# Sparse attention with a gated feed-forward network: the scores of six steps formed eight steps ahead and kept in DRAM

## The chip, the cores and the metric

One core of one Trainium2 chip runs the whole program. The metric is the device time in microseconds of one execution; the kernel before was run three times, and the median of these is the time before.

## The reference

```python
def _attn_ref(q, k, v):                      # (8, 8, 576, 64) each
    scores = scale * np.matmul(q, k.transpose(0, 1, 3, 2))
    kth = np.partition(scores, -32, axis=-1)[..., -32:-31]
    scores = np.where(scores >= kth, scores, -1e9)
    attn = np.exp(scores - np.max(scores, axis=-1, keepdims=True))
    attn = attn / (np.sum(attn, axis=-1, keepdims=True) + 1e-09)
    return np.matmul(attn, v)

def _moe_ref(x, w_gate, w_val, w_out):       # x (4608, 512), 512 -> 1536 -> 512
    gate = 1.0 / (1.0 + np.exp(-(x @ w_gate)))
    return gate * (x @ w_val) @ w_out
```

In each row of the scores only the 32 largest of 576 count; the output of all heads goes through the feed-forward network.

## The kernel before, in words

The attention is cut into 160 steps. A step is 128 rows of a pair of heads (two score rows of 576 per partition), or the last 64 rows of both heads. Steps are numbered n = 0, 1, ...; the first batch has steps 0 to 7 (row tiles 0 and 1 of the four pairs of heads), 8 to 15 (tiles 2 and 3) and 16 to 19 (the rest). In the names of tiles, `s_2_1` is tile 2 of pair 1, which is step 10; steps 10 to 15 are `2_1`, `3_1`, `2_2`, `3_2`, `2_3`, `3_3`.

A step goes through these stations. `begin` (L633) runs `scores` (L300): two groups of matmuls `pss` on TensorE (L310), each into the one buffer of the PSUM pool `ps_s`, and after each an eviction to `s` by ScalarE (L314). `select` (L389) finds a threshold on VectorE: `cand` (L407) and `tops` and `leads` (L412, L414) take the 24 largest; from the last of these ScalarE marks in `under` (L422) what is below it, GpSimd multiplies the marks into `u` (L429, closed by L430), and VectorE takes `kths` (L437), the 32nd value. ScalarE forms the exponentials `e` (L344), VectorE masks and sums them (L349). `turn` (L440) transposes them on TensorE (`pt`, L448) with evictions to `ring` (L454), `weigh` (L478) multiplies by the values (`po`, L496).

Beside this runs the feed-forward network in float32 split into a high and a low part. Its weights are loaded raw (`wraw`), split once on ScalarE, VectorE (`wbits`, `wpower`, L203 to L205), GpSimd (`wsplit`, L209) and TensorE (`wrest`, L217 to L219), and written to DRAM, from where later units read them.

The loop of `run` (L616) writes, for every n, the matmuls of the scores of step n + 2, of the transposes of step n - 2 and of the feed-forward network in chunks; TensorE keeps exactly this order. The order on the other engines and on SyncE's queue is made by a scheduler from the program. Up to `OPEN` = 9 there is no feed-forward work to interleave; the first weights are split then. Scores have four buffers (`bs`), so the scores of step n + 4 go where step n's lay, once step n is masked.

Of the kernel before, what the change touches and what calls it, by code (L numbers as in the profile page):

```python
# [10 lines left out]
F32 = mybir.dt.float32  # L11
# [6 lines left out]
AF = mybir.ActivationFunctionType  # L18
# [5 lines left out]
SHRINK = 2.0**-60  # L24
# [6 lines left out]
def tile_topk_attention_then_gated_ffn(  # L31
# [8 lines left out]
    nc = tc.nc  # L40
    P = 128
    B, H, _, S = k.shape
    D = P // 2
    HALF = S // 2
    NP = H // 2
# [3 lines left out]
    FG = NE = NP  # L49
    NF = 2 * n_w // 3  # L50
    NG = NF // FG
    SCALE = 1.0 / 8.0
# [9 lines left out]
    groups = [(b, half) for b in range(B) for half in (halves[b % 2] if b else opening)]  # L62
# [6 lines left out]
    def size(i):  # L69
        return P if i < NT else REM  # L70
# [12 lines left out]
    WHOLE = 1  # L83

    OPEN = NP * 2 + 1
    PINNED, BACK = 3, 6
    KEPT = 3

# [13 lines left out]
    dram = ctx.enter_context(tc.tile_pool(name="dram", bufs=1, space=bass.MemoryType.DRAM))  # L102
# [21 lines left out]
    pools = {}  # L124
# [24 lines left out]
    def urgent():  # L149
        return tc.high_priority() if stated else ExitStack()  # L150

    for name, bufs in (("w", 3), ("f2", 3), ("f4", 3), ("fg", FG + 1)):
        pools[name] = ctx.enter_context(tc.tile_pool(name=name, bufs=bufs))


    order = list(range(FG))
# [4 lines left out]
    stored, splits, waiting, fetched, ticks, evicted, due, later, pinned, raw_loads = set(), {}, [], {}, [0], [], [], [], [], []  # L161
# [10 lines left out]
    def load(dst, src_, late=False):  # L172
        with tc.issue_after(raw_loads[max(0, len(raw_loads) - BACK)]) if late and raw_loads else ExitStack():
            ins = nc.sync.dma_start(dst, src_)
        if pinned:
            tc.keep_in_program_order(ins)
        return ins
# [54 lines left out]
    def first_weights(at):  # L232
        for t in order[at : at + 3]:
            if t in fetched:
                continue
            if t in order[:KEPT]:
                fetched[t] = splits[t]
                continue
            if t in stored:
                fetched[t] = stored_weight(t, "first")  # L240
                continue
            while due:
                next_front()
            due.extend([(t, 0), (t, 1)])
            next_front()
            fetched[t] = splits[t]
# [53 lines left out]
    def scores(s, qs, ks, i, nm):  # L300

        J = 2 if i < NT else 1
        K = D if len(qs) == 1 else P
        if K == D and J == 2:
            for half in range(2):
                ps = ps_s.tile([P, 2, 512], F32, tag="s", name=f"pss_{nm}_{half}")
                c = slice(half * HALF, (half + 1) * HALF)
                for j in range(J):
                    rows = slice(j * D, (j + 1) * D)
                    nc.tensor.matmul(  # L310
                        ps[:, j, :HALF], qs[0][rows, j * P : (j + 1) * P], ks[0][rows, c], start=True, stop=True
                    )
                with urgent():
                    evicted.append(nc.scalar.activation(s[:, :, c], ps[:, :, :HALF], AF.Copy, scale=SCALE * SHRINK))  # L314
                yield
            return
        for j in range(J):
            ps = ps_s.tile([P, 2, 512], F32, tag="s", name=f"pss_{nm}_{j}")
            for half in range(2):

                parts = [(j, 0, HALF, half * HALF)]
                if i == NT:

                    m = S - REM - HALF
                    parts += [(1, 0, HALF, REM)] if half == 0 else [(1, 0, m, REM + HALF), (1, m, REM, 0)]
                todo = [(x, part) for part in parts for x in qs]
                for t, (x, (h, o, n, k0)) in enumerate(todo):
                    nc.tensor.matmul(  # L328
                        ps[:, half, o : o + n],
                        x[:K, h * P : (h + 1) * P],  # L330
                        ks[h][:K, k0 : k0 + n],
                        start=t == 0,
                        stop=t == len(todo) - 1,
                    )
            with urgent():
                nc.scalar.activation(  # L336
                    s[:, j].rearrange("p (a n) -> p a n", a=2), ps[:, :, :HALF], AF.Copy, scale=SCALE * SHRINK
                )
            yield
# [276 lines left out]
    def run(general):  # L616
# [11 lines left out]
        def fetch_values(m):  # L628
            if 0 <= m < len(steps) and steps[m][2] == groups[steps[m][0]][1][0] and steps[m][:2] not in values:
                g, p, _ = steps[m]  # L630
                values[g, p] = load_values(groups[g][0], p, f"{mark}{g}_{p}")

        def begin(m):  # L633
            if m < len(steps):
                g, p, i = steps[m]
                nm = f"{mark}{groups[g][0]}_{i}_{p}"
                staged[m] = bs.tile([P, 2, S], F32, tag="s", name=f"s_{nm}")
                yield from scores(staged[m], qs.pop(m), keys[groups[g][0], p], i, nm)

        def ask(m):  # L640
            if m < len(steps):
                g, p, i = steps[m]
                qs[m] = load_queries(groups[g][0], i, p)

# [140 lines left out]
        for n in range(len(steps) + 3):  # L785
            splitting = not general and len(fronts) > 0
            if pinned and n == PINNED:
                pinned.pop()
            if n == 0:
                fetch_keys(2)  # L790
                ask(AHEAD)
            if splitting:
                split_front(*fronts.pop(0))
            if n == OPEN and not general:
                first_weights(0)
            if n == 0:
                for m in (1, *range(3, KEYS)):
                    fetch_keys(m)
                for m in range(AHEAD + 1, ASK):
                    ask(m)  # L800
            if later and (general or n >= 2 * NP):
                load(*later.pop(0))
            fetch_values(n if n < starts[GATHER - 1] else n - 2)
            fetch_keys(n + KEYS)
            ask(n + ASK)
            goal = 0 if n < OPEN else max(at - BEHIND, np.interp(at, *zip(*PACE))) * per_row
            first = begin(n + AHEAD)
            second = turned(n - 2) if 2 <= n < len(steps) + 2 and (general or n != OPEN) else iter(())
            if region is None:
                for _ in first:  # L810
                    pass
                choose(n)
                more(goal)
                for _ in second:
                    pass
                if 2 <= n < len(steps) + 2:
                    weighed(n - 2)
            else:
                if n == OPEN - 1:
                    weighed(n - 3)  # L820
                if n == OPEN:
                    weighed(n - 3)
                    weighed(n - 2)
                choose(n)
                if n == OPEN + 1:
                    del standing["cand"], standing["tops"]
                    opened.clear()
                if n == OPEN + NP:
                    standing.clear()
                third = iter(())  # L830
                chunks = [first, second, second, first, None, second]
                if n == OPEN - 1:
                    third = turned(n - 1)
                    chunks = [second, second, second, first, third, third, third, first]
                if n == OPEN:
                    chunks = [first, None, None, first]
                begun = work
                for t, chunk in enumerate(chunks):
                    ticks[0] += 1
                    if not fronts and not splitting:  # L840
                        if waiting and ticks[0] - waiting[0][4] > 3:
                            split_back()
                        if due and len(waiting) < 3:
                            next_front()
                    if chunk is not None:
                        next(chunk, None)
                        while unfinished and t == 0:
                            weighted(*unfinished.pop(0))
                    elif 3 <= n:
                        weighed(n - 3)  # L850
                    if t == 2 and splitting and len(waiting) > 1:
                        split_back()
                    if n != OPEN or t > 0:
                        more(begun + (goal - begun) * (t + 1) / len(chunks))
                for _ in third:
                    pass
                for chunk in (first, second):
                    for _ in chunk:
                        pass
            if 2 <= n < len(steps) + 2:  # L860
                at += size(steps[n - 2][2]) / NP
# [77 lines left out]
```

## Time and profile before

| what | value |
|---|---|
| time, median of three runs (lowest to highest) | 1569.1 us (1567.16 to 1569.84) |
| the profiled execution's own time | 1569.45 us |
| its span, first to last instruction | 1567.7 us |
| TensorE matmuls busy | 1502.3 us, 96% |
| TensorE weight loads busy | 1311.4 us, 84% |
| VectorE busy | 1289.9 us, 82% |
| ScalarE busy | 1149.4 us, 73% |
| GpSimd busy | 1106.3 us, 71% |
| mean granted clock of TensorE | 0.989 |

The span leaves 1.75 us of the own time outside. Busy shares are means over stages: a stage has its own fullest engine, and time is lost or won there.

### The profile page before, as it was taken

How to read it: one execution, taken by the hardware profiler on the slowest of the kernel's cores; microseconds unless marked ns; L12 is line 12 of the kernel's file. 1: busy time of each engine (PE TensorE's matmuls, PEld its weight loads, DVE VectorE, ACT ScalarE, POOL GpSimd, SP SyncE). 2: the span in 40 equal slices, each digit the busy share in tenths (PEclk: the TensorE clock that was granted, in tenths of full speed). 3: DMA queues.
4: the chain of work that ended last, by engine and by line, in shares of the span. 5: the costliest groups of instructions: out<-in, count | busy, mean ns of one | idle time of the engine just before them, and what ended most of it. 6: DMA issues, size and time to landing. Idle time of an engine off the chain costs nothing.

```text
span 1567.7 us, 33618 instructions
## 1 busy us (share of the span) xinstructions
PE 1502.3 (96%) x10242; PEld 1311.4 (84%) x10242; DVE 1289.9 (82%) x5996; ACT 1149.4 (73%) x2519; POOL 1106.3 (71%) x1656
## 2 busy tenths in 40 slices
PE   5688999999999999999999999999999999999998
PEld 2355668988898899888898899888898899889897
DVE  7999987899999788999989788999988788998001
ACT  6888987888777777787777777787777778776221
POOL 4758897698786876897676876887675876774312
PEclk9899999999999999999999999999999999999999
DMA  6436888777665675665565676575565676564575
GB/s 204 152 123 220 280 285 299 257 269 271 229 221 192 231 268 202 207 241 205 199 213 192 230 271 207 204 253 205 199 211 191 229 248 207 197 214 169 210 272 185
DMA packets 96239, 347.34 MB, mean 222 GB/s; under 512 B 13104, under 2 KB 33584, under 8 KB 68272
## 3 DMA queue, kind: packets, MB, share of 16 engines
q1 hardware_dynamic: 90864, 326.22, 60.3%
q10 hardware_dynamic: 5184, 18.88, 3.1%
q8 instruction: 83, 1.36, 0.3%
q14 instruction: 108, 0.88, 0.2%
HBM read 316.60 MB, written 28.45 MB: 220 GB/s over the span
## 4 chain that ended last, share of the span: by engine, by line
PE 68%; DVE 15%; POOL 7%; ACT 6%; issue 3%; DMA 2%; SPq 0%; ACTq 0%; POOLq 0%; DVEq 0%
PE pz L557 10%; PE pz L558 10%; PE pz L559 10%; PE po L496 8%; PE pss L328 8%; PE pt L448 6%; PE po L581 5%; PE po L582 5%; PE po L583 5%; DVE e L349 3%; POOL u L429 3%; DVE cand L407 3%; DVE kths L437 3%; POOL wsplit L209 1%; ACT under L422 1%
## 5 line engine op out<-in xcount | busy, mean ns | idle before, releaser
L429 POOL TENSOR_TENSOR u<-s,under 128x288 f32<-128x288 f32 x576 | 425.3, 762 | 128.1 <-ACT under L422 123.3
L557 PE MATMUL pz<-xh,w 128*128 128x384 f32 (+1 forms) x1152 | 404.4, 351 | 0.0
L407 DVE MAX8 cand<-s 128x8 f32<-128x72 f32 x2304 | 353.4, 217 | 38.8 <-ACT s L336 26.7
L559 PE MATMUL pz<-xh,w 128*128 128x384 f32 (+1 forms) x1152 | 377.4, 328 | 0.0
L558 PE MATMUL pz<-xl,w 128*128 128x384 f32 (+1 forms) x1152 | 376.9, 327 | 0.0
L422 ACT ACTIVATE under<-s,leads 128x576 fp8e4<-128x576 f32 x288 | 222.4, 773 | 102.3 <-DVE leads L412 94.0
L349 DVE SCALAR_TENSOR_TENSOR e<-s,kths,e 128x576 f32<-128x576 f32 x288 | 282.4, 987 | 14.8 <-ACT e L344 14.4
L437 DVE MAX8 kths<-u 128x8 f32<-128x584 f32 x288 | 219.3, 762 | 71.0 <-POOL u L430 68.5
L569 POOL TENSOR_TENSOR gl<-gf,gh 128x384 fp32r<-128x384 f32 (+1 forms) x156 | 156.6, 1004 | 120.3 <-ACT gh L568 117.4
L557 PEld LDWEIGHTS pz<-xh,w 128*128 128x128 f32 x1152 | 217.0, 188 | 5.6 <-DVE tops L412 1.1
L344 ACT ACTIVATE e<-s,st 128x576 f32<-128x576 f32 x288 | 208.9, 770 | 16.0 <-PE pt L448 8.5
L558 PEld LDWEIGHTS pz<-xl,w 128*128 128x128 f32 x1152 | 217.7, 189 | 0.8
L559 PEld LDWEIGHTS pz<-xh,w 128*128 128x128 f32 x1152 | 216.5, 188 | 0.0
L454 ACT ACTIVATE ring<-pt 128x384 f32<-128x384 f32 x336 | 163.1, 495 | 56.2 <-PE pt L448 54.8
L448 PE MATMUL pt<-ident,e 128*128 128x128 f32 x1152 | 192.0, 276 | 6.9 <-ACT ring L454 6.9
L448 PEld LDWEIGHTS pt<-ident,e 128*128 128x128 f32 x1152 | 147.5, 142 | 38.7 <-ACT ring L454 10.5
L581 PE MATMUL po<-w,gh 128*128 128x512 f32 x408 | 173.1, 424 | 1.2 <-DVE gf L567 1.2
L336 ACT ACTIVATE s<-pss 128x576 f32<-128x576 f32 x256 | 164.0, 641 | 9.1 <-PE pss L328 8.5
L328 PE MATMUL pss<-k,qh 128*128 128x288 f32 (+2 forms) x588 | 162.2, 294 | 8.6 <-ACT s L336 8.4
L582 PE MATMUL po<-w,gl 128*128 128x512 f32 x408 | 161.2, 395 | 2.8 <-POOL gl L569 2.8
L567 DVE SCALAR_TENSOR_TENSOR gf<-gf,pz 128x384 f32<-128x384 f32 (+1 forms) x156 | 79.7, 511 | 99.9 <-PE pz L559 87.8
L583 PE MATMUL po<-w,gh 128*128 128x512 f32 x408 | 161.2, 395 | 0.0
(114 smaller groups left out, 3314.0 us busy)
## 6 DMA issues: line engine op xcount, KB each, us to landing
w<-ws SPq DMA_DIRECT2D x216, 1024.0 KB
v<-in_v_dram SPq DMA_DIRECT2D x68, 320.0 KB
wraw<-in_w_dram SPq DMA_DIRECT2D x36, 512.0 KB
ws<-wsplit ACTq DMA_DIRECT2D x36, 512.0 KB
qraw<-in_q_dram SPq DMA_DIRECT2D x140, 128.0 KB
kraw<-in_k_dram SPq DMA_DIRECT2D x56, 288.0 KB
out_dram<-acc SPq DMA_DIRECT2D x36, 256.0 KB
invb<-rows SPq DMA_DIRECT2D x66, 128.0 KB
```

What stands on the lines that cost most here:

```text
L328: nc.tensor.matmul(ps[:, half, o : o + n], x[:K, h * P : (h + 1) * P], ks[h][:K, k0 : k0 + n], start=t == 0, stop=t == len(todo) - 1,)
L349: nc.vector.scalar_tensor_tensor(e[:, j], s[:, j], kth[j], e[:, j], op0=ALU.is_ge, op1=ALU.mult, accum_out=st[:, 4 + j : 5 + j])
L407: nc.vector.max(cand[:, j, 8 * g : 8 * g + 8], s[:, j, g * SEG : (g + 1) * SEG])
L429: nc.gpsimd.tensor_tensor(u[:, j, c], s[:, j, c], under[:, j, c], op=ALU.mult)
L437: nc.vector.max(kths[:, at[j] : at[j] + 8], u[:, j])
L448: nc.tensor.transpose(pt[:, c], ef[:, k0 : k0 + P], ident)
L557: nc.tensor.matmul(ps[:, R], wt[:, u, 0, d], xh[:, R], start=d == 0, stop=False)
L558: nc.tensor.matmul(ps[:, R], wt[:, u, 0, d], xl[:, R], start=False, stop=False)
L559: nc.tensor.matmul(ps[:, R], wt[:, u, 1, d], xh[:, R], start=False, stop=d == NP - 1)
L581: nc.tensor.matmul(outs[r], gh, wh, start=f == 0, stop=False)
L582: nc.tensor.matmul(outs[r], gl, wh, start=False, stop=False)
L583: nc.tensor.matmul(outs[r], gh, wl, start=False, stop=f == FG - 1)
```

## The change

Steps 10 to 15 (`SAVED`) have their scores formed in the turns n = 2 to 7, one step's in each, eight steps ahead. `save` loads their queries into a pool of its own, runs `scores` into a pool `es` of three buffers, and stores the result to DRAM from ScalarE's queue. In the turns n = 8 to 13 `begin` reads it back into the buffer of `bs` in place of forming it, and `ask` no longer loads these queries. The chunks of the turns 2 to 7 become nine in place of six. The pools of the feed-forward network are opened at `OPEN`, where the two new pools are closed.

```diff
+    SAVED = range(OPEN + 1, OPEN + 2 * NP - 1)
...
-    for name, bufs in (("w", 3), ("f2", 3), ("f4", 3), ("fg", FG + 1)):
-        pools[name] = ctx.enter_context(tc.tile_pool(name=name, bufs=bufs))
+    pools["w"] = ctx.enter_context(tc.tile_pool(name="w", bufs=3))
+    kept = ExitStack()
+    kept_pools = {n: kept.enter_context(tc.tile_pool(name=n, bufs=bufs, side="right")) for n, bufs in (("es", 3), ("eq", 3))}
+    saved = {}
+
+    def feed_forward_pools():
+        kept.close()
+        for name, bufs in (("f2", 3), ("f4", 3), ("fg", FG + 1)):
+            pools[name] = ctx.enter_context(tc.tile_pool(name=name, bufs=bufs, side="right"))
...
+        def save(m):
+            if m in SAVED and not general:
+                g, p, i = steps[m]
+                b = groups[g][0]
+                nm = f"{b}_{i}_{p}_saved"
+                whole = kept_pools["eq"].tile([P, 2 * P], F32, tag="q", name=f"q_{nm}")
+                load(whole, q[b, i, p])
+                s = kept_pools["es"].tile([P, 2, S], F32, tag="s", name=f"s_{nm}")
+                yield from scores(s, (whole,), keys[b, p], i, nm)
+                saved[m] = dram.tile([P, 2, S], F32, tag=f"s{m}", name=f"saved_{m}")
+                nc.scalar.dma_start(saved[m], s)
...
                 staged[m] = bs.tile([P, 2, S], F32, tag="s", name=f"s_{nm}")
+                if m in saved and not general:
+                    nc.sync.dma_start(staged[m], saved.pop(m))
+                    return
                 yield from scores(staged[m], qs.pop(m), keys[groups[g][0], p], i, nm)
...
-            if m < len(steps):
+            if m < len(steps) and (general or m not in SAVED):
...
             if n == OPEN and not general:
+                feed_forward_pools()
                 first_weights(0)
...
                 chunks = [first, second, second, first, None, second]
+                early = save(n + OPEN - 1)
+                if n + OPEN - 1 in SAVED and n < OPEN - 1:
+                    chunks = [first, second, early, second, first, None, second, early, early]
```

The order of TensorE in the turn n = 4, from the first scores of step 6 (`pss_0_3_0`) to the second; `pt_0_1` are the transposes of step 2, `wrest` belongs to a weight split. Before:

```order
L310 MATMUL pss_0_3_0_663<-k_3_6_410,q_0_3_414 128x288 x2
L448 MATMUL pt_0_1_0_667<-ident,e_0_1_420 128x128 x3
L448 MATMUL pt_0_1_1_672<-ident,e_0_1_420 128x128 x3
L217 MATMUL wrest_1_677<-wbits_1_500,ident 128x512
L218 MATMUL wrest_1_677<-wsplit_395,minus 128x512
L219 MATMUL wrest_1_677<-wsplit_395,minus 128x512
L310 MATMUL pss_0_3_1_683<-k_3_6_410,q_0_3_414 128x288 x2
```

Now, where lines stand eight to ten further down:

```order
L318 MATMUL pss_0_3_0_686<-k_3_6_407,q_0_3_411 128x288 x2
L458 MATMUL pt_0_1_0_690<-ident,e_0_1_417 128x128 x3
L318 MATMUL pss_2_2_saved_698<-k_2_4_254,q_2_2_saved 128x288 x2
L225 MATMUL wrest_1_702<-wbits_1_510,ident 128x512
L226 MATMUL wrest_1_702<-wsplit_392,minus 128x512
L227 MATMUL wrest_1_702<-wsplit_392,minus 128x512
L458 MATMUL pt_0_1_1_708<-ident,e_0_1_417 128x128 x3
L318 MATMUL pss_0_3_1_713<-k_3_6_407,q_0_3_411 128x288 x2
```

The first half of the scores of step 12 stands between the two halves of step 6, in the same PSUM buffer, and one group of transposes moves behind the weight split; the second half of step 12 comes at the end of the turn.

The order of VectorE in step 7 (`1_3`), from the row after its last `leads` to its first `kths<-u_1_3`. Before:

```order
L407 MAX cand_2_0_1051<-s_2_0_875 128x8 x5
L364 RECIPROCAL st_1_2_727<-st_1_2_727 128x2
L407 MAX cand_2_0_1051<-s_2_0_875 128x8
L437 MAX kths<-u_0_3_829 128x8
L407 MAX cand_2_0_1051<-s_2_0_875 128x8 x8
L501 TENSOR_TENSOR xf_3_0_913<-po_3_902,ring 128x128 x2
L407 MAX cand_2_0_1051<-s_2_0_875 128x8 x2
L204 SCALAR_TENSOR_TENSOR wbits_0_1368<-wraw_0_924,wbits_0_1368 128x512
L437 MAX kths<-u_0_3_829 128x8
L349 SCALAR_TENSOR_TENSOR e_0_3_828,st_0_3_826<-s_0_3_662,kths,e_0_3_828 128x576
L205 TENSOR_SCALAR wpower_0_1369<-wbits_0_1368 128x512
L437 MAX kths<-u_1_3_943 128x8
```

Now, from the two `leads` of step 7 on:

```order
L422 MAX leads<-cand_1_3_996 128x8 x2
L417 MAX cand_2_0_1120<-s_2_0_922 128x8 x8
L447 MAX kths<-u_1_3_1001 128x8 x2
L211 TENSOR_SCALAR wbits_0_1423<-wbits_0_1423 128x512
L212 SCALAR_TENSOR_TENSOR wbits_0_1423<-wraw_0_984,wbits_0_1423 128x512
L213 TENSOR_SCALAR wpower_0_1424<-wbits_0_1423 128x512
L417 MAX cand_2_0_1120<-s_2_0_922 128x8 x8
```

The thresholds and the masking of step 6 have moved ahead of the `leads` of step 7, the weight split behind its `kths`; what stands between `leads` and `kths` is eight `cand`. Before, a `wbits` (L203) and a small operation stood between the two `leads` as well.

SyncE's queue after the first weights have been asked for (`w_first`). Before:

```order
L229 DMA w_first_1255<-ws_129 128x2048
L174 DMA q_3_3_1424<-in_q_dram 128x256
L174 DMA wraw_1_1489<-in_w_dram 128x1024
L174 DMA wraw_0_1517<-in_w_dram 128x1024
L174 DMA wraw_1_1573<-in_w_dram 128x1024
```

Now:

```order
L237 DMA w_first_1319<-ws_129 128x2048
L661 DMA s_2_2_1382<-saved_745 128x1152
L182 DMA wraw_1_1539<-in_w_dram 128x1024
L182 DMA wraw_0_1567<-in_w_dram 128x1024
L661 DMA s_3_2_1530<-saved_854 128x1152
L182 DMA wraw_1_1619<-in_w_dram 128x1024
L661 DMA s_2_3_1737<-saved_982 128x1152
```

The scores of steps 12, 13 and 14 are read back between the loads of raw weights; the query load has gone.

## Rows read from the trace of the kernel before

**Rows 1.** Windows: PE, PEld, DVE, ACT, POOL busy; clock, DMA share, GB/s.
```profile
20.00:95.00 75.00, 55.73 (x256) 29.37 (x256) 71.10 (x330) 59.21 (x122) 44.18 (x70) 0.89 0.52 162
95.00:180.00 85.00, 76.25 (x424) 54.11 (x421) 81.36 (x309) 74.09 (x154) 68.55 (x97) 0.96 0.65 223
180.00:240.00 60.00, 54.76 (x293) 38.81 (x292) 47.79 (x144) 49.69 (x103) 55.58 (x79) 1.00 0.79 276
240.00:1567.00 1327.00, 1307.57 (x9253) 1186.10 (x9251) 1078.16 (x5143) 955.22 (x2124) 931.96 (x1389) 1.00 0.64 223
```

**Rows 2.** Waits of VectorE, 20 to 95 us: total us, times, longest.
```profile
DVE cand L407 <- ACT s L314: 1.7, 2, 1.0
...
DVE kths L437 <- POOL u L430: 0.4, 1, 0.4
```

**Rows 3.** Waits of TensorE, 20 to 95 us.
```profile
PE pss L310 <- ACT s L314: 15.1, 7, 3.6
```

**Rows 4.** Windows, line L310 alone: PE, PEld busy; clock, DMA share, GB/s.
```profile
89.00:157.00 68.00, 9.64 (x48) 3.82 (x48) 0.95 0.53 183
```

**Rows 5.** Windows, line L314 alone: ACT busy; clock, DMA share, GB/s.
```profile
89.00:157.00 68.00, 7.11 (x11) 0.95 0.53 183
```

**Rows 6.** Timeline of TensorE: start us, us, instruction, count, idle before.
```profile
28.77 1.33 PE L310 MATMUL pss<-k,q 64*128 64x288 f32 x4 [1.93 <-ACT s L314]
...
60.24 0.76 PE L310 MATMUL pss<-k,q 64*128 64x288 f32 x4
```

**Rows 7.** Chain of waits, 14 to 302 us: start us, us, what.
```profile
23.64 0.48 DVE wbits L203
...
34.66 0.46 ACT under L422
...
40.44 0.04 DVE kths L437
...
41.12 0.41 DVE wpower L205
...
46.38 6.79 DMA wraw<-in_w_dram
...
66.71 0.67 DVE wbits L204
...
95.52 0.49 DVE xf L501 x2
96.01 1.49 DVE cand L407 x11
97.49 0.67 DVE kths L437
...
99.63 0.72 DVE e L349 x2
...
301.26 4.68 DMA w<-ws
```

**Rows 8.** Timeline of VectorE, around 92 us.
```profile
92.46 0.22 DVE L412 MAX8 leads<-cand 128x8 f32<-128x64 f32 x1
```

**Rows 9.** Timeline of ScalarE, around 93 us.
```profile
92.91 0.77 ACT L422 ACTIVATE under<-s,leads 128x576 fp8e4<-128x576 f32 x1
```

**Rows 10.** Timeline of GpSimd, 92 to 98 us.
```profile
93.84 2.67 POOL L429 TENSOR_TENSOR u<-s,under 128x288 f32<-128x288 f32 x4 [1.42 <-ACT under L422]
96.47 0.46 POOL L430 TENSOR_TENSOR u<-over,sums 128x16 f32<-128x16 f32 x2
```

**Rows 11.** Waits of VectorE, 95 to 200 us.
```profile
DVE kths L437 <- POOL u L430: 3.8, 4, 2.0
...
DVE cand L407 <- ACT s L314: 0.7, 1, 0.7
```

**Rows 12.** The page's DMA issues: count, KB each.
```profile
w<-ws SPq DMA_DIRECT2D x216, 1024.0 KB
...
wraw<-in_w_dram SPq DMA_DIRECT2D x36, 512.0 KB
```

More of the change, by code (lines that the diff above doesn't have):

```diff
@@ L313, in scores @@
                 with urgent():
-                    evicted.append(nc.scalar.activation(s[:, :, c], ps[:, :, :HALF], AF.Copy, scale=SCALE * SHRINK))
+                    out_ = nc.scalar.activation(s[:, :, c], ps[:, :, :HALF], AF.Copy, scale=SCALE * SHRINK)
+                    if not nm.endswith("saved"):
+                        evicted.append(out_)
                 yield
```

## Prediction

> **What bounds the kernel now.** I read the busy time by stage first, then who waits for whom in the first stage, then the chain of waits for durations. By stage [rows 1]: up to 20 us things fill up. From 20 to 95 us (the opening, steps 0 to 8, no feed-forward work yet) VectorE is busy 71.10 of 75 us, TensorE only 55.73. From 95 to 180 us VectorE is busy 81.36 of 85 us and TensorE 76.25. From 180 to 240 us GpSimd is the fullest, 55.58 of 60 us. From 240 us to the end TensorE is busy 1307.57 of 1327 us. So a delay or a gain that reaches 240 us passes almost whole to the end, and before it the engine to watch is VectorE: what it does not lose, no other engine can win. In the opening it hardly waits: 1.7 us in two waits for scores and 0.4 us for a threshold (`kths`) [rows 2]. TensorE waits much there, 15.1 us in seven waits, and all of it for ScalarE to empty the one PSUM buffer of scores [rows 3].
>
> **What moves.** 24 matmuls, seen as 48 records, leave the stretch from 89 to 157 us, where they take 9.64 us [rows 4], and 12 evictions with them (11 fall inside this stretch, 7.11 us [rows 5]). Both go into steps 2 to 7. A group of four records lasts 0.76 us at the full clock of 2.4 GHz and 1.33 us at 1.2 GHz [rows 6]; the granted clock in the opening is 0.89 on the mean [rows 1]. So TensorE takes on 9 to 16 us, of which 75 - 55.73 = 19.3 us are free, and ScalarE, busy 59.21 of 75 us [rows 1], about 7 us. By busy time there is room, and in the same way nothing is won behind: from 89 to 157 us the removed work lies beside a VectorE that is busy 96%. I cost the removal at nothing for that reason. If VectorE were not the cover, it would be worth up to 9.64 us (first rival).
>
> **The loss: cover on VectorE.** The order of VectorE shows the price. After the last `leads` of a step its thresholds need `under` on ScalarE and five operations on GpSimd. What VectorE has to do meanwhile is its cover. The change puts an eviction behind `under` in ScalarE's order and two more turns of the one PSUM buffer into each step, so the next step's scores come later, and in the new order VectorE stands with less to do. For step 7 before: two `leads`, 16 `cand`, two `kths`, `xf`, one `wbits` of each kind, `wpower`, one `e`, two small ones. By the chain's durations [rows 7] that is 0.3 + 16 x 1.49/11 (2.2) + 2 x 0.67 + 0.49 + 0.48 + 0.67 + 0.41 + 0.72 + 0.2 = 6.8 us. After: two `leads` and eight `cand`, 0.3 + 1.1 = 1.4 us. Worked out in the same way from the whole order, steps 4, 5, 6 have 8.8, 7.0 and 8.0 us before and 4.2, 1.4 and 2.3 us after; steps 0 to 3 keep 5.8 us or more.
>
> What the loop needs: undisturbed, `leads` starts at 92.46 us [rows 8], `under` at 92.91 [rows 9], four `u` run from 93.84 and the first closing `u` ends near 96.7 [rows 10], so 4.2 us. Disturbed by a weight split, `under` starts at 34.66 and `kths` at 40.44 us [rows 7], 5.8 us, with the 0.45 us ahead of it 6.2 us. Step 7 then waits 2.8 to 4.8 us, step 5 the same, step 6 1.9 to 3.9 us, step 4 0 to 2.0 us: together 7.5 to 15.5 us. I take values near the undisturbed end, because the new order has no weight split between the `u` of steps 5 and 7: 2.8 + 2.8 + 2.4 (step 6 has an `inv` and an eviction in between) + 1.0 (step 4, an eviction and a `wsplit`) = **+9.0 us**. The 1.7 us of waits for scores [rows 2] go, since `cand` now comes later: **-1.7 us**.
>
> **The gain behind the opening.** In steps 9 to 15 the cover grows, since scores no longer wait for TensorE's turn: from 7.5, 5.5, 9.0, 10.2, 5.0, 5.6, 4.2 to 9.5, 7.9, 11.2, 10.8, 10.0, 6.8, 6.1 us. VectorE's waits from 95 to 200 us are 3.8 us in four for `u` and 0.7 us for scores [rows 11]. At best all 4.5 us go, at worst none; with three of seven covers formerly near the 4.2 to 6.2 us needed and all above 6 now, I take **-3.4 us**.
>
> **The read-back.** Each of the six loads (576 KB) waits on SyncE's queue until the step four before has been masked, and behind it stand raw weights (the order above). The raw weights in front of it wait for VectorE too, but for splits that stand earlier in its order. From the end of `e` of step 9 to `cand` of step 13 VectorE has 4.3 us of work, from step 8 to step 12 6.4 us, for the other loads more. The trace has no such load. Nearest rows: 1024 KB of weights in 4.68 us, 512 KB of raw weights in 6.79 us [rows 7], sizes in [rows 12]. With about 0.3 us to issue, step 13 waits 0.7 to 2.8 us and step 12 up to 0.7; nothing, if a half-empty set of DMA engines (busy 0.65 [rows 1]) is quicker. I take **+0.7 us**, by the larger transfer. The Trainium skill, "DMA: Bandwidth & Descriptors", sections "Specifications" and "Anatomy of one DMA", gives some 2 us of fixed cost and 368 GB/s; an estimate from that page is 2 + 1.6 = 3.6 us, which would hide all six and make the sum 0.7 us less. The rows speak for more, but under other traffic.
>
> **At nothing.** The six stores are issued on ScalarE's queue beside its work, and land while steps 3 to 9 run. The six query loads only change places. The pools of the feed-forward network now lie where the saved scores lay, so their first writes wait for the last store, which has the whole of step 8 to land; should it be late, the first Tanh waits and TensorE behind it, a few us at most. The reads add 3.5 MB to a DMA share of 0.65 to 0.79 [rows 1].
>
> **Sum.** 9.0 - 1.7 - 3.4 + 0.7 = +4.6 us by 240 us, where TensorE takes over and passes it on. The profiled execution took 1569.45 us, 0.35 us above the median of the three runs, so the median should go from 1569.1 to **1573.7 us**. Bounds of the terms alone: from 7.5 - 1.7 - 4.5 = +1.3 us, with 3 us more taken back in the 12.2 us that VectorE idles from 180 to 240 us [rows 1] -1.7 us, to 15.5 - 0 + 3.5 = +19 us, with all four steps disturbed at once, which I think rare.
>
> **Rivals.** (1) *Faster.* The stretch from 89 to 240 us is limited by TensorE and ScalarE after all, and VectorE is only kept busy by an order that follows them. It decides if the covers of steps 4 to 7 cost less than the relief. For it: TensorE is busy 76.25 of 85 us and VectorE stands in the chain only in turns with others. Against it: 96% busy. Price: the 9.64 us [rows 4] at most, and half of it if the other half lies beside other work as now, so about -5 us without the loss and 1564 us. The Trainium skill, "Perfetto Trace Analysis", section "Optimization Strategy", says that kernels with several regimes may gain from interleaving them, which is what is done here; by that rule the time falls, the rows say that both regimes share VectorE. 13%.
> (2) *No change.* The added waits of the opening are given back whole, because VectorE's idle time, 3.6 us from 95 to 180 and 12.2 us from 180 to 240 us [rows 1], take them up: 1569. 13%.
> (3) *Much slower.* The one PSUM buffer becomes the bound of the opening: 12 more turns at the 15.1/7 = 2.2 us that a turn waits now [rows 3] are 26 us, of which the 4 us of TensorE's idle time that are no such wait, and half of the rest, hide; about +12 us, 1581. For it: ScalarE's order puts evictions behind `under`, which waits for VectorE. Against it: VectorE reaches the next `cand` after its wait for `kths`, by when the scores are out. The Trainium skill, "Perfetto Trace Analysis", section "Matmuls", wants matmul groups to rotate through PSUM banks so that evictions overlap, and speaks against adding groups here; the 15.1 us agree. 14%.
> That the change does not do what it says I rule out: the order shows the matmuls in their new places.
>
> **Numbers.** The forecast holds 60%: of that 48 slower by over 0.2% (3.1 us, about what a measurement of this kernel can tell from no change) and 12 within it. With the rivals: faster 13%, within 25%, slower 62%. Range 1566 to 1582 us: it takes in the forecast, no change, most of the third rival and the nearer part of the first.
>
> **What would show it.** VectorE's waits for `u` in the first 105 us rise from 0.4 to some 9 us, by about 2.5 us a step in steps 5 to 7, with the boundary at 95 us about 7 us later; from there to 200 us they nearly vanish; `cand` of step 13 waits for a DMA by about 1 us; TensorE's first full slice comes about 5 us later. The forecast is wrong if VectorE's idle time in the opening stays under 5 us, or if the stretch from the first feed-forward matmul to 240 us shrinks by more than 6 us.

## The result and the profile after

The changed kernel takes 1592.2 us (median, 1590.5 to 1593.7) against 1569.2 us for the kernel before on the same chip: ratio 1.0149, 95% interval 1.0131 to 1.0166, so 23.1 us slower. The forecast was 1573.7 us, with a range of 1566 to 1582: the direction was right, the loss five times as large. The profiled execution took 1591.46 us, its span is 1589.4 us.

Where the time went is told by the places where VectorE scales a finished weighing (`xf`). The last one of the opening starts at 115.48 us, before at 95.52 [rows 7]: 20.0 us later. Behind it, a place that both traces show is a run of ten score matmuls (`pss` x10) in the stretch where TensorE is full: it starts at 262.73 us, before at 241.24, 21.5 us later. The whole span is 21.7 us longer. So nearly all of the loss arises in the opening, and nothing is given back behind it.

Windows of the changed kernel, with the columns of [rows 1]:

```profile
20.00:116.00 96.00, 66.46 (x302) 34.43 (x303) 72.32 (x333) 68.45 (x135) 43.13 (x72) 0.80 0.57 183
116.00:200.00 84.00, 67.10 (x366) 49.74 (x366) 78.78 (x304) 65.66 (x136) 66.01 (x95) 0.92 0.69 233
200.00:262.00 62.00, 57.35 (x306) 41.35 (x305) 50.38 (x147) 52.48 (x110) 56.38 (x82) 1.00 0.83 282
```

VectorE does the same work up to the boundary, 72.32 us against 71.10 in [rows 1], but in 96 us where it had 75. Its waits in that stretch (us in all, times, longest):

```profile
DVE xf L511 <- PE po L507: 9.1, 2, 8.3
DVE kths L447 <- POOL u L440: 7.5, 3, 2.9
DVE cand L417 <- ACT s L322: 4.7, 2, 4.0
DVE wbits L211 <- ACT wbits L209: 1.7, 1, 1.7
```

They add up to 23.0 us. Before, up to 96 us, so that the wait ahead of the last `xf` of the opening is counted there too, the 1.7 us for `cand` and 0.4 for `kths` of [rows 2] stand beside

```profile
DVE xf L501 <- PE po L497: 1.8, 2, 1.2
...
DVE wbits L203 <- ACT wbits L201: 0.3, 1, 0.3
```

which makes 4.2 us. The difference in waiting, 18.8 us, and the 1.2 us of more work (72.32 - 71.10) are the 20.0 us by which the boundary moved: VectorE is the engine to watch, as the prediction had it, but little more than a third of its new waits (7.5 - 0.4 = 7.1 us) is the one that was forecast. Their places, in VectorE's timeline (start, us, instruction, in brackets the idle time ahead):

```profile
40.02 1.18 DVE L417 MAX8 cand<-s 128x8 f32<-128x72 f32 x8 [3.97 <-ACT s L322]
...
67.62 0.77 DVE L447 MAX8 kths<-u 128x8 f32<-128x584 f32 x1 [2.91 <-POOL u L440]
...
79.36 0.77 DVE L447 MAX8 kths<-u 128x8 f32<-128x584 f32 x1 [1.94 <-POOL u L440]
...
91.50 1.57 DVE L447 MAX8 kths<-u 128x8 f32<-128x584 f32 x2 [2.60 <-POOL u L440]
...
106.59 0.49 DVE L511 TENSOR_TENSOR xf<-po,ring 128x128 f32<-128x128 f32 x2 [8.26 <-PE po L507]
```

The three `kths` are those of steps 5, 6 and 7. The other two, 12.2 us together, wait for work that comes out of TensorE. What TensorE waited for up to 116 us:

```profile
PE pss L318 <- ACT s_saved L322: 15.4, 5, 5.3
PE pss_saved L318 <- ACT s L322: 7.7, 8, 2.5
PE pss L318 <- ACT s L322: 5.2, 2, 2.6
```

That is 28.3 us for the one PSUM buffer of scores, against 15.1 in [rows 3]. The largest single one shows how it comes about. TensorE's timeline, and then ScalarE's in the same place:

```profile
40.04 0.76 PE L318 MATMUL pss_saved<-k,q_saved 64*128 64x288 f32 x4 [0.16 <-ACT s L322]
46.12 1.33 PE L318 MATMUL pss<-k,q 64*128 64x288 f32 x4 [5.33 <-ACT s_saved L322]
```

```profile
39.34 0.65 ACT L322 ACTIVATE s<-pss 128x576 f32<-128x576 f32 x1 [0.65 <-PE pss L318]
39.88 0.66 ACT L209 ACTIVATE wbits<-wraw 128x512 f32<-128x512 f32 x1
40.44 0.66 ACT L215 ACTIVATE wsplit<-wraw 128x512 fp32r<-128x512 uint32 x1
40.98 0.60 ACT L464 ACTIVATE ring<-pt 128x512 f32<-128x512 f32 x1
41.46 0.78 ACT L432 ACTIVATE under<-s,leads 128x576 fp8e4<-128x576 f32 x1
...
42.22 0.78 ACT L432 ACTIVATE under<-s,leads 128x576 fp8e4<-128x576 f32 x1
...
42.98 1.45 ACT L354 ACTIVATE e<-s,st 128x576 f32<-128x576 f32 x2
44.31 0.67 ACT L209 ACTIVATE wbits<-wraw 128x512 f32<-128x512 f32 x1
44.87 0.67 ACT L215 ACTIVATE wsplit<-wraw 128x512 fp32r<-128x512 uint32 x1
45.43 0.64 ACT L322 ACTIVATE s_saved<-pss_saved 128x576 f32<-128x576 f32 x1
```

The saved half is done at 40.8 us, but its eviction stands in ScalarE's order behind seven operations that start only after that (from `ring` to the last `wsplit`), and runs at 45.43. Until then the buffer is full, the next step's own half can't start, and the transposes and weighings behind it in TensorE's order stand too. The same pattern makes the 8.26 us; in the chain of waits (start, us, what):

```profile
97.18 0.55 ACT s_saved L322
...
97.77 0.78 PE pss L318 x4
...
98.58 0.66 ACT s L322
...
99.28 0.76 PE pss_saved L318 x4
100.03 1.07 PE wrest L225 x2
...
101.13 0.68 ACT wbits L209
...
102.70 0.66 ACT s L322
...
103.40 0.76 PE pss_saved L318 x4
104.16 0.36 PE po L506
```

The one buffer is handed on from a saved half to an own half to a saved half, each time through ScalarE, and `po`, which VectorE waits for, comes behind the last of them.

### The profile page after: what moved, and what is told of

It is laid out like the page before. It is cut to its first block, busy times and chain, and to the rows that moved or that the text cites. A ratio compares the mean times of both kernels' runs of the same rounds, so it can differ in the third digit from the quotient of the medians.

```text
span 1589.4 us, 33647 instructions
## 1 busy us (share of the span) xinstructions
PE 1506.2 (95%) x10242; PEld 1314.3 (83%) x10242; DVE 1292.5 (81%) x5996; ACT 1153.0 (73%) x2519; POOL 1103.3 (69%) x1656
## 4 chain that ended last, share of the span: by engine, by line
PE 65%; DVE 17%; POOL 7%; ACT 5%; issue 3%; DMA 3%; SPq 0%; POOLq 0%; DVEq 0%; ACTq 0%
PE pz L567 10%; PE pz L569 9%; PE pz L568 9%; PE pss L338 7%; PE po L506 7%; PE pt L458 5%; PE po L591 5%; PE po L593 5%; PE po L592 5%; DVE e L359 4%; DVE cand L417 4%; DVE kths L447 3%; POOL u L439 3%; DVE cand L424 1%; DMA wraw<-in_w_dram 1%
## 5 line engine op out<-in xcount | busy, mean ns | idle before, releaser
L359 DVE SCALAR_TENSOR_TENSOR e<-s,kths,e 128x576 f32<-128x576 f32 x288 | 285.8, 999 | 14.4 <-ACT e L354 13.9
```

Of the source, the lines that this page charges most:

```text
L359: nc.vector.scalar_tensor_tensor(e[:, j], s[:, j], kth[j], e[:, j], op0=ALU.is_ge, op1=ALU.mult, accum_out=st[:, 4 + j : 5 + j])
```

## The experiments

The theory after the result (A): the loss is made in the opening, by the turns of the one PSUM buffer, through ScalarE's order; the work removed behind the opening was worth nothing. Its rivals: the extra evictions or matmuls themselves, the place of the saved halves in the order, the stores or the read-back, and single steps that cost more than the others. Each run's difference is taken to the kernel before on the same chip (in the table's order: 1569.15 us for the changed kernel, 1569.35 for the four runs after it, 1568.42 for the next four, 1568.54 for the next three, 1566.78 for the last). The two runs without stores that still evict, and the one with four saved steps, have two executions each, the others four or more. The last two columns are from VectorE's timeline: the start of the `xf` that ends the opening, and of the next one. The scheduler makes the order of VectorE and ScalarE anew for each run, so a difference between two runs holds the change of order with it.

| run | against before, us | ratio, 95% interval | end of opening | next `xf` |
|---|---|---|---|---|
| before | | | 95.5 | 144.4 |
| changed kernel | +23.1 | 1.0131 to 1.0166 | 115.5 | 167.6 |
| no relief | +21.9 | 1.0123 to 1.0156 | 120.6 | 167.8 |
| relief only | +5.8 | 1.0025 to 1.0059 | 94.7 | 148.3 |
| saved halves late | +22.6 | 1.0131 to 1.0165 | 117.0 | 168.6 |
| own PSUM buffer | +8.1 | 1.0033 to 1.0070 | 105.5 | 154.4 |
| no relief, no store | +24.5 | 1.0128 to 1.0187 | 120.7 | 168.3 |
| the same, own buffer | +12.1 | 1.0050 to 1.0108 | 110.1 | 157.2 |
| the same, no eviction | +5.4 | 1.0018 to 1.0050 | 101.8 | 148.5 |
| four saved steps | +15.2 | 1.0069 to 1.0128 | 112.0 | 162.4 |
| pools only | -0.9 | 0.9984 to 1.0004 | 95.1 | 144.0 |
| two buffers, none saved | +2.3 | 1.0004 to 1.0024 | 93.2 | 146.8 |
| no transfer in place of the removed | -0.2 | 0.9987 to 1.0006 | 93.4 | 142.3 |
| changed kernel without read-back | +22.4 | 1.0132 to 1.0179 | 116.2 | 164.9 |

**No relief.** Steps 10 to 15 form their own scores again, the opening stays as changed.

```
-                if m in saved and not general:
-                    nc.sync.dma_start(staged[m], saved.pop(m))
-                    return
...
-            if m < len(steps) and (general or m not in SAVED):
+            if m < len(steps):
```

> The opening as in the changed kernel (six steps' scores formed ahead and stored), but steps 10 to 15 form their own scores again from their own queries and nothing is read back, so 24 matmuls and 12 evictions are done twice. Theory A (the whole loss arises in the opening, by turns of the one PSUM buffer that other work stands behind, and the removed work behind it was worth nothing): about the changed kernel's time, 1590 to 1596 us, with the last xf of the opening near 115 us as there. Theory B (the loss is the opening's, but the removal gave back 3 to 5 us behind it, as forecast): 1595 to 1598 us. Theory C (the read-back or its traffic is part of the loss): below 1588 us.

1591.2 us, as the changed kernel: 24 matmuls and 12 evictions done twice cost nothing against the read-back in their place. B is out. C isn't supported, but this run alone doesn't free the read-back: its opening ends 5.1 us later (step 10's own scores fall into step 8), which the expectation under A did not have, and it has made that up by the next `xf`.

**Relief only.** Nothing is formed ahead; steps 10 to 15 read back the stored scores of step 3.

```
-                if m in saved and not general:
-                    nc.sync.dma_start(staged[m], saved.pop(m))
+                if m in SAVED and not general:
+                    nc.sync.dma_start(staged[m], saved[0])
...
+                if m == 3 and not general:
+                    saved[0] = dram.tile([P, 2, S], F32, tag="s0", name="saved_0")
+                    nc.scalar.dma_start(saved[0], staged[m])
...
-                early = save(n + OPEN - 1)
-                if n + OPEN - 1 in SAVED and n < OPEN - 1:
-                    chunks = [first, second, early, second, first, None, second, early, early]
```

> Nothing is formed ahead; the scores of step 3 are stored once, and steps 10 to 15 read that tile back in place of forming their own (their own scores are left out of the computation). This prices the removal and the read-back alone, on an opening like that of the kernel before. Theory A (removal worth nothing, read-back hidden): 1567 to 1570 us. Theory B (forecast: waits behind the opening vanish, less 0.7 us of read-back): 1565 to 1567 us. The first rival of the prediction (TensorE and ScalarE limit the stretch from 89 to 240 us): 1557 to 1564 us. Theory C (read-back costs): over 1571 us.

1575.2 us: slower by 5.8, which no theory of gain allows. The opening is that of before (94.7), the next `xf` comes 3.9 us late.

**No transfer.** The relief-only edit without the store, where the read-back is replaced by the scores of step 9, still in their buffer.

```
+                if m in SAVED and not general:
+                    staged[m] = saved[0]
+                    return
...
+                if m == OPEN and not general:
+                    saved[0] = staged[m]
```

> As the relief-only run (1575.2 us), but without any transfer: steps 10 to 15 select from the scores of step 9, which stay in their buffer, so their own scores are left out of the computation, and neither matmuls, evictions, queries nor read-backs stand in their place. Theory G (the read-back on SyncE's queue costs: raw weights stand behind it): 1567 to 1570 us or below. Theory H (what cost 5.8 us there is the order that follows when scores are there early: cand is drawn ahead of thresholds and weight splits on VectorE): 1573 to 1577 us again.

1568.3 us. So removing the matmuls, evictions and queries is worth 0.2 us, within its interval nothing, and the read-back (with the one store) cost 6.0 us on that opening, in the range of G. H is not enough: here too the scores are there early, and VectorE takes 96 `cand` between the two `xf`, as in the relief-only run (before, 80). VectorE waits only once, 1.2 us, for the transfer itself. SyncE's queue shows what the reads do there. Relief only, the issues of reads and raw weights from 103 to 170 us (start, us, count at the end):

```profile
103.86 0.33 SPq L661 DMA_DIRECT2D s<-saved  x1
106.48 1.42 SPq L182 DMA_DIRECT2D wraw<-in_w_dram  x2
108.01 0.37 SPq L661 DMA_DIRECT2D s<-saved  x1
113.30 8.95 SPq L182 DMA_DIRECT2D wraw<-in_w_dram  x2
123.93 0.33 SPq L661 DMA_DIRECT2D s<-saved  x1
126.12 0.33 SPq L182 DMA_DIRECT2D wraw<-in_w_dram  x1
130.45 0.33 SPq L661 DMA_DIRECT2D s<-saved  x1
133.12 13.44 SPq L182 DMA_DIRECT2D wraw<-in_w_dram  x4
...
152.43 17.52 SPq L182 DMA_DIRECT2D wraw<-in_w_dram  x4
```

Without the transfer:

```profile
104.28 27.64 SPq L182 DMA_DIRECT2D wraw<-in_w_dram  x7
...
140.16 21.35 SPq L182 DMA_DIRECT2D wraw<-in_w_dram  x6
```

The thirteenth raw weight is issued by 169.95 us with the read-back and by 161.51 without: the reads wait 10.5 us in the queue for the masking that frees their buffer (`e`, in three waits), and the weights behind them come 8 us later. VectorE feels it late. Up to the next `xf` it does not stand idle, beyond the 1.2 us: it is busy 52.42 us where the run without the transfer has 48.95, with weight splits and thresholds that the order puts ahead there. From that `xf` to 246 us it then waits 8.9 us for weight splits (`wbits`), without the transfer 3.9 us up to 241. That the late weights are the cause fits these rows; no run takes the delay out alone and leaves the order as it was.

**The changed kernel without its read-back.** The same edit on the changed kernel.

> The changed kernel without its read-back: six steps' scores are formed ahead and stored as there, but steps 10 to 15 select from the scores of step 9, which stay in their buffer (their own are left out of the computation). If the read-back costs in the changed kernel what it cost on the opening of the kernel before (1575.2 against 1568.3 us, 6.9 us): 1583 to 1587 us, with the weighing after the opening's last one near 164 us in place of 167.6. If a VectorE that is late anyway hides it: 1590 to 1593 us.

+22.4 us against +23.1, with intervals that cover each other: in the changed kernel the read-back costs too little to be told from nothing by the times. The time lies between the two expected ranges, on a chip whose kernel before takes 1566.78 us; only the sign that the first one named, the next `xf` near 164 us, came (164.9). The stretch from the end of the opening to that `xf` is 48.7 us in place of 52.1, but VectorE is busy 48.70 us of it here and 51.73 us in the changed kernel, so 3.0 us are work that the order puts ahead, not waiting. At the `pss` x10 of the result section 1.6 us are left of it (261.12 against 262.73). That a late VectorE hides the rest is not shown.

**Saved halves late.** Both halves behind the step's own work.

```
-                    chunks = [first, second, early, second, first, None, second, early, early]
+                    chunks = [first, second, second, first, None, second, early, early, early]
```

> The changed kernel with both halves of the saved scores at the end of each step's order, behind its transposes and its weighing, in place of one half between the step's own halves. Theory A1 (the place matters: the step's own second half and the weighing stand behind a turn of the saved scores): VectorE's waits for scores and for po shrink, 1578 to 1586 us. Theory A2 (each turn costs wherever it stands, since the one buffer is handed on through ScalarE's queue): within 4 us of the changed kernel, 1588 to 1596 us.

1592.0 us. The place doesn't matter (A2): the waits only change places. VectorE waits 12.0 us for `po` of steps 4 and 5 where it was 8.3.

**An own PSUM buffer** of two banks for the saved scores, until the feed-forward work begins.

```
+    pools["pf"] = opening.enter_context(tc.tile_pool(name="ps_w", bufs=1, space=bass.MemoryType.PSUM))
+    pools["px"] = opening.enter_context(tc.tile_pool(name="ps_x", bufs=1, space=bass.MemoryType.PSUM))
...
         kept.close()
+        opening.close()
+        pools["pf"] = ctx.enter_context(tc.tile_pool(name="ps_f", bufs=3, space=bass.MemoryType.PSUM))
...
-                ps = ps_s.tile([P, 2, 512], F32, tag="s", name=f"pss_{nm}_{half}")
+                ps = (pools["px"] if nm.endswith("saved") else ps_s).tile([P, 2, 512], F32, tag="s", name=f"pss_{nm}_{half}")
```

> The changed kernel with a PSUM buffer of their own for the saved scores in the opening (two banks taken from the three of the weight remainders, which get one until the feed-forward work begins). Theory A3 (the one PSUM buffer is the bound: the third rival of the prediction): the step's own scores no longer wait for the saved ones' evictions, VectorE's waits for scores (4.7 us) and for po (9.1 us) go, those for the thresholds (7.5 us) stay: 1576 to 1582 us. Theory A4 (ScalarE's order: the evictions and what they stand behind cost, whatever buffer they empty): 1586 to 1593 us.

1577.4 us: 15.0 us of the 23.1 are gone. VectorE's waits from 20 to 105 us are now

```profile
DVE xf L515 <- PE po L511: 6.2, 2, 6.1
DVE cand L421 <- ACT s L326: 2.8, 2, 2.2
DVE wbits L215 <- ACT wbits L213: 1.5, 1, 1.5
DVE kths L451 <- POOL u L444: 0.8, 1, 0.8
```

A3 holds in its time, but not in its parts: the 7.5 us for `kths`, which should have stayed, fell to 0.8, while most of the wait for `po` stayed. In step 7 sixteen `cand`, a weight split and an `xf` stand between `leads` and `kths` here, where the changed kernel has eight `cand`: the next step's scores are there as cover.

**The ladder.** Three more runs take the opening apart, all with steps 10 to 15 forming their own scores. First without stores:

```
-                saved[m] = dram.tile([P, 2, S], F32, tag=f"s{m}", name=f"saved_{m}")
-                nc.scalar.dma_start(saved[m], s)
```

> As the run without relief (saved scores formed in the opening, steps 10 to 15 form their own again), but the saved scores are thrown away: no store of 576 KB a step on ScalarE's queue. Prices the stores. In the run without relief the last weighted sum of the opening is scaled at 120.6 us, in the kernel before at 95.5. Theory D (the 3.5 MB of stores delay the raw weights, whose arrival stands in the chain twice, 6.1 and 3.7 us): 5 us or more earlier than 120.6, time 1583 to 1587 us. Theory A (turns of the PSUM buffer and ScalarE's order): within 2 us, time 1589 to 1593 us.

1592.9 us: the stores cost nothing that shows (A). Then with the own buffer of above as well:

> As the run without stores, with a PSUM buffer of their own for the saved scores in the opening. Against the run without stores it prices the shared buffer, without any DMA traffic of the stores. Theory A3 (the shared buffer is the larger part): 10 to 15 us faster than the run without stores, 1575 to 1580 us. Theory A4 (ScalarE's queue, which still empties 12 more buffers, is the larger part): less than 6 us faster.

1580.6 us: sharing the buffer costs 12.4 us (24.5 - 12.1), without any store or read-back in play. TensorE still waits for the saved scores' own buffer, up to 111 us

```profile
PE pss_saved L322 <- ACT s_saved L326: 11.0, 6, 4.6
```

Then without evictions:

```
+                if nm.endswith("saved"):
+                    yield
+                    continue
                 with urgent():
```

> As the run with their own buffer and no stores, but the saved scores are never emptied from PSUM: only the 24 matmuls, their queries' loads and the changed pools are left in the opening. Against the run before it this prices the 12 evictions (7.7 us of ScalarE's time). Theory A4 (evictions in ScalarE's order): back to 1570 to 1572 us. Theory E (TensorE's own order: matmuls that wait for a late query and the lower clock hold the transposes and weighings behind them): 1574 to 1578 us, near the run with evictions, with a TensorE wait for the first saved query of some microseconds.

1573.8 us, between A4 and E, 0.2 us under E: the evictions cost 6.7 us (12.1 - 5.4; the intervals meet at 1.0050, so that its size is rough), and matmuls and query loads still cost 5.4. With the evictions went TensorE's waits for their buffer, so this is not ScalarE's time alone. TensorE waits 1.8 us for the first saved query here, and VectorE 4.5 us for `kths`, 1.8 of it in step 7 and 2.7 in step 8. The control, with the pools as in these runs and no step saved:

```
-    SAVED = range(OPEN + 1, OPEN + 2 * NP - 1)
+    SAVED = range(0)
```

> No step is saved: the kernel before, but with the feed-forward pools opened at step 9 and, until then, one bank for the weight remainders in place of three and an idle two-bank buffer beside the one for scores. The control for the runs with a buffer of their own. Theory A (what the matmuls-only run still lost, 5.4 us, is TensorE's order and the queries' loads): 1567 to 1571 us. Theory F (the lost 5.4 us are the single bank of the remainders or the moved pools): 1573 to 1575 us.

1567.6 us: the pools cost nothing, so the remainder, 6.3 us (5.4 + 0.9, from two chips and so rough), is the matmuls and loads, with the order that follows from them. How it divides between TensorE's order, a late query and the clock stays open.

**Four saved steps** in place of six (the range of saved steps ends two earlier).

> The changed kernel with only steps 10 to 13 saved, formed in steps 2 to 5; steps 14 and 15 form their own scores in their old place. If each saved step costs the same: two thirds of the loss, 1582 to 1585 us. If the last two cost more than their share, since they stand ahead of the weighing of steps 4 and 5 that VectorE waited 8.3 us for: 1577 to 1581 us. If the first two do (queries that come late, a raw weight on the chain): 1586 to 1590 us.

1583.6 us, +15.2, two thirds of 23.1 (15.4): 3.8 us a step in either kernel, so the last two cost no more than their share. The interval, 10.8 to 20.1 us, is wide, and the first four are not told apart.

**Two buffers, none saved.** The control's spare buffer serves the steps' own second halves.

> As the control, but the second two-bank buffer serves the steps' own scores: their two halves alternate between the two buffers during the opening. No step is saved. If VectorE is the bound of the opening (busy 71.1 of 75 us before, waiting 3.1 us): TensorE's 15.1 us of waits for the buffer go and the time hardly moves, 1565 to 1569 us. If the one buffer is what spaces out the opening of the kernel before, too: 1558 to 1564 us.

1570.9 us, 2.3 us slower (3.2 against the control), above both expected ranges, so nothing is gained; why it is slower stays open. TensorE's 15.1 us of waits for the buffer [rows 3] are down to

```profile
PE pss L323 <- ACT s L327: 0.6, 1, 0.6
```

but those of the transposes for `ring` rise from 5.4 to 10.3 us. The opening ends 2.4 us earlier, and the next `xf` comes 2.4 us later. So TensorE's waits for the buffer in the kernel before cost nothing: VectorE is the bound there. No run of this study beat the kernel before.

## Why the prediction was wrong

*The bound.* Right: VectorE limits the opening, and what it loses reaches the end. Its added waits are 18.8 of the 20.0 us by which the boundary moved.

*The loss of cover, +9.0.* Nearly the right size as a sum: 7.5 us measured, in steps 5, 6 and 7 2.91, 1.94 and 2.60 for 2.8, 2.4 and 2.8 forecast, in step 4 none, where 1.7 us of waiting for a weight split stands just ahead. The mechanism held: step 7 has two `leads` and eight `cand` as cover, as read from the order. Of the reasons that the prediction gave for it, the turns of the one buffer weigh most, since with a buffer of their own for the saved scores 0.8 us is left.

*The waits for scores, -1.7.* **This is the step that failed.** It rests on "`cand` now comes later", and the third rival was refused by the same thought: "VectorE reaches the next `cand` after its wait for `kths`, by when the scores are out". The scores were not out. The waits for them rose from 1.7 to 4.7 us, 3.0 more where 1.7 less were forecast, and the wait of `xf` for `po`, for which the sum had no term, rose from 1.8 to 9.1 us. Both stand behind a TensorE that waits before a full buffer. In the sum, scores that come late should have been followed through TensorE's whole order, to the transposes and weighings that stand behind them.

*"By busy time there is room."* It failed as well: 19.3 us of idle TensorE and 15.8 us of idle ScalarE did not take in the added work, because TensorE's idle time was mostly waits for one buffer, and an eviction holds it by its place in ScalarE's order (the 5.33 us above). Not all of it was such waits, as the prediction has it: the same list has 5.4 us in eight waits of the transposes for `ring`. Measured: evictions, with the waits for their buffer, 6.7 us, matmuls and loads 6.3 us.

*The third rival.* Its mechanism is what happened, and its price, "about +12 us" (its own terms give 11), is near the 12.4 us that sharing the buffer costs in the ladder. It was wrong in being a rival: the evictions and matmuls cost beside it, and the lost cover is in good part its own doing. The waits of TensorE for the buffer rose by 13.2 us, half of the 26 that it counted for 12 turns; that half of them would hide was a guess from no row, so the nearness is partly luck.

The Trainium skill, "Perfetto Trace Analysis", section "Matmuls", wants independent groups of matmuls to rotate through PSUM banks so that emptying one overlaps the next. Where groups were added, the runs agree: an own buffer gave back 15.0 us. Where none were, a second buffer removed the waits and gained nothing (+2.3 us).

*The gain behind the opening, -3.4.* None: the run without a transfer is 0.2 us from the kernel before, and its interval (-2.0 to +0.9 us) leaves out the 3.4. The first rival falls with it. The rule that it cited from the Trainium skill, "Perfetto Trace Analysis", section "Optimization Strategy", that interleaving regimes may gain, is not borne out here: both stretches were full of VectorE's work, 71.10 of 75 us in the opening and 64.50 of 68 us from 89 to 157 (95%, not the 96 of the prediction).

*The read-back, +0.7.* In the changed kernel VectorE waits 0.4 us for it in one place, `cand` of step 13 as forecast, and the times can't tell it from nothing. The chain has that read:

```profile
129.77 4.65 DMA s<-saved
```

That is close to the larger transfer of 4.68 us, by which the term was taken. The estimate of 3.6 us from the Trainium skill, "DMA: Bandwidth & Descriptors", was too short for it; the fixed cost in it stands there under "Anatomy of one DMA" for DMAs of the GpSimd path, and this one goes out from SyncE. But the mechanism was incomplete. I counted the wait of `cand` and named the raw weights behind the reads on SyncE's queue without a price; on the opening of before the read-back cost 6.0 us, of which that wait is 1.2.

*At nothing.* The stores and the pools were right.

*The signs.* The waits for `u` and the wait of step 13 came about as named, and nothing that was to show the forecast wrong came up, yet the loss was five times as large. What told them apart is the boundary, 20.0 us later in place of 7.

## What to carry over

Idle time of an engine is room for new work only if it doesn't consist of waits for the resource that the new work uses: look at what ends the idle time, and follow each added turn of a buffer through the in-order queue of the engine that empties it, up to the next instruction that the bounding engine waits for. Removed work that lies beside a full engine can be worth nothing, as 9.64 us of it were here; take it out alone, with nothing in its place, before paying for it elsewhere. When two mechanisms of loss can both hold, add them instead of choosing one.

## What was not expected

The granted clock of TensorE in the opening fell although it got more matmuls. From 36 us to the end of the opening, before and then changed (columns of [rows 1]):

```profile
36.00:95.50 59.50, 43.99 (x224) 23.65 (x226) 55.97 (x255) 48.71 (x101) 37.12 (x60) 0.86 0.42 139
```

```profile
36.00:115.50 79.50, 56.35 (x274) 29.61 (x273) 55.85 (x251) 56.69 (x111) 34.69 (x59) 0.81 0.49 169
```

The means from 20 us on, 0.89 in [rows 1] and 0.80, can't be compared: in the first 34 us of the trace before, and 28 us of the changed one, the column reads 1.00 beside groups of four records that take 1.33 us, the one at 28.77 us in [rows 6] among them. The group after the 5.33 us of waiting took 1.33 us at a granted clock of 0.50 (1.2 GHz), the group just ahead of that wait 0.76 us at 1.00. The changed opening has 15 waits for the buffer (28.3 us), the one before seven (15.1 us): more matmuls came with more idle stretches. What the lower clock costs was not measured.

A transfer that VectorE waited 1.2 us for made the kernel 6.0 us slower; the traces point to what stood behind it on its queue, and to the order that changed with it.
